# Low-rank attention and a feed-forward layer: attention of the next half batch between feed-forward matmuls, transposed, two heads per matmul, with loads that convert

## The chip, the cores and the metric

The kernel runs on one core of a Trainium2 chip. Time is device microseconds; the engines are PE (matmuls), ACT (activations), DVE (elementwise), POOL (here it issues the loads) and SP (it can issue transfers too). All inputs and the output are fp32; matmuls run in bf16 with fp32 sums.

## The reference

```python
batch, n_heads, seq, head_dim = (8, 8, 1024, 64);  k_proj = 64       # attention
n_tokens, d_model, d_ff = (8192, 512, 2048)                          # feed-forward

k_proj = np.einsum('ks,bhsd->bhkd', E, k)
v_proj = np.einsum('ks,bhsd->bhkd', F, v)
scores = scale * np.matmul(q, k_proj.transpose(0, 1, 3, 2))          # scale = 1/8
scores = scores - np.max(scores, axis=-1, keepdims=True)
attn = np.exp(scores)
attn = attn / (np.sum(attn, axis=-1, keepdims=True) + 1e-09)
attn_out = np.matmul(attn, v_proj)

x = attn_out.transpose(0, 2, 1, 3).reshape(B * S, H * D)
h = x @ w_in
g = h * (1.0 / (1.0 + np.exp(-1.702 * h)))
out = g @ w_out
```

## The kernel before, in words

It has two stages, one after the other. Stage one loops over the 8 batches. For each it loads Q, K and V in 8 chunks of 128 tokens (`kvf`, 256 KB each, all 8 heads side by side), converts each chunk to bf16 on DVE (`kvb`, L83, L103, L105), transposes Q per head on PE (L86, `qtb`), and sums K and V over the 1024 tokens against E and F (L106, L107, `kp_ps`, `vp_ps`). K's projection is transposed per head (`kpT`), V's gets a column of ones (`vp_ext`), which makes the softmax denominator come out of the same matmul. Then for each head and each half of the tokens (512): scores as 64 x 512 (L126), Exp on ACT (L129), the product with `vp_ext` (L131), a copy (L133), four transposes back to tokens on rows (L137), a reciprocal of the denominators (L140, 128 x 4), and a multiply into `x_all` (L143), which holds all 8192 tokens in SBUF.

Stage two loops over 16 blocks of 512 tokens: 16 transposes of `x_all` to `xT` (L160, L161); for each of 16 slices of the hidden layer four matmuls (L167) and one Gelu (L173) into `gT`; then 64 matmuls of the second layer (L176) into four PSUM banks, one copy of them on DVE (L183) and a 1 MB store (L184).

The weights are loaded in fp32 in stage one and converted on DVE (L60, L64). All transfers are issued by POOL, in one queue. The order on each engine is made by a scheduler from dependencies and buffer counts (most pools have two buffers, the PSUM pool of the second layer one).

Of the kernel before, what the change touches and what calls it, by code (L numbers as in the profile page):

```python
# [15 lines left out]

@with_exitstack
def kernel(ctx, tc, q, k, v, E, F,
                                                     moe_w_in, moe_w_out, out):
    nc = tc.nc  # L20
# [16 lines left out]
    ps_sm = ps_sm_ctx.__enter__()
# [3 lines left out]
    identf = consts.tile([P, P], F32)  # L41
    nc.vector.tensor_copy(identf, ident)

    ET = consts.tile([P, SC, KP], BF16)
    FT = consts.tile([P, SC, KP], BF16)
    w_in_sb = consts.tile([P, KC, DFF], BF16)
    w_out_sb = consts.tile([P, FC, DM], BF16)
    with tc.tile_pool(name="init", bufs=1) as init:
        for src, dst in [(E, ET), (F, FT)]:
            E_f = init.tile([KP, S], F32, name="ef_f32")  # L50
            nc.gpsimd.dma_start(out=E_f, in_=src)
            for sc in range(SC):
                ef_ps = ps_sm.tile([P, P], F32, name="sc_ps")
                nc.tensor.transpose(ef_ps[:, :KP], E_f[:, sc * P:(sc + 1) * P], identf[:KP, :KP])
                nc.vector.tensor_copy(dst[:, sc, :], ef_ps[:, :KP])
# [10 lines left out]
    x_all = consts.tile([P, NCHUNK, DM], BF16)

    GW = 4 * P

    ps_a_ctx = tc.tile_pool(name="ps_a", bufs=1, space=bass.MemoryType.PSUM)  # L70
    ps_a = ps_a_ctx.__enter__()
    for b in range(B):
        ci0 = b * SC
        qT = qpool.tile([D, H, S], BF16, name="qtb")
        qTv = qT.rearrange("d h (sc p) -> d h sc p", p=P)
        for sc in range(SC):
            qch_f = kvw.tile([P, H * D], F32, name="kvf")
            nc.gpsimd.dma_start(  # L78
                out=qch_f.rearrange("p (h d) -> p h d", h=H),
                in_=q[b, :, sc * P:(sc + 1) * P, :].transpose([1, 0, 2]),  # L80
            )
            qch = kvw.tile([P, H * D], BF16, name="kvb")
            nc.vector.tensor_copy(qch, qch_f)  # L83
            qt_ps = ps_sm.tile([D, H, P], BF16, name="qt_ps")
            for h in range(H):
                nc.tensor.transpose(qt_ps[:, h, :], qch[:, h * D:(h + 1) * D], ident)  # L86
            nc.vector.tensor_copy(qTv[:, :, sc, :], qt_ps)  # L87

        kp_ps = ps_a.tile([KP, H * D], F32, name="kp_ps")
        vp_ps = ps_a.tile([KP, H * D], F32, name="vp_ps")  # L90
        for sc in range(SC):
            kch_f = kvw.tile([P, H * D], F32, name="kvf")
            nc.gpsimd.dma_start(  # L93
                out=kch_f.rearrange("p (h d) -> p h d", h=H),
                in_=k[b, :, sc * P:(sc + 1) * P, :].transpose([1, 0, 2]),
            )
            vch_f = kvw.tile([P, H * D], F32, name="kvf2")
            nc.gpsimd.dma_start(  # L98
                out=vch_f.rearrange("p (h d) -> p h d", h=H),
                in_=v[b, :, sc * P:(sc + 1) * P, :].transpose([1, 0, 2]),  # L100
            )
            kch = kvw.tile([P, H * D], BF16, name="kvb")
            nc.vector.tensor_copy(kch, kch_f)  # L103
            vch = kvw.tile([P, H * D], BF16, name="kvb2")
            nc.vector.tensor_copy(vch, vch_f)  # L105
            nc.tensor.matmul(kp_ps, ET[:, sc, :], kch, start=(sc == 0), stop=(sc == SC - 1))  # L106
            nc.tensor.matmul(vp_ps, FT[:, sc, :], vch, start=(sc == 0), stop=(sc == SC - 1))  # L107

        vp_ext = work.tile([KP, H, D + 1], BF16, name="vp_ext")
        nc.vector.memset(vp_ext[:, :, D:D + 1], 1.0)  # L110
        kp_sb = work.tile([KP, H, D], F32, name="kp_sb")
        nc.vector.tensor_copy(kp_sb.rearrange("k h d -> k (h d)"), kp_ps)
        for h in range(H):
            nc.vector.tensor_copy(vp_ext[:, h, :D], vp_ps[:, h * D:(h + 1) * D])

        kpT_sb = work.tile([D, H, KP], BF16, name="kpT")
        for h in range(H):
            t_ps = ps_sm.tile([D, P], F32, name="qt_ps")
            nc.tensor.transpose(t_ps[:, :KP], kp_sb[:, h, :], identf[:KP, :KP])
            nc.vector.tensor_copy(kpT_sb[:, h, :], t_ps[:, :KP])  # L120

        for h in range(H):
            for sg in range(S // GW):
                col0 = sg * GW
                sc_ps = ps_sm.tile([KP, GW], F32, name="sc_ps")
                nc.tensor.matmul(sc_ps, kpT_sb[:, h, :], qT[:, h, col0:col0 + GW],  # L126
                                 start=True, stop=True)
                expT = small.tile([KP, GW], BF16, name="expT")
                nc.scalar.activation(expT, sc_ps, AF.Exp, scale=scale)  # L129
                out_ps = ps_sm.tile([D + 1, GW], F32, name="out_ps")  # L130
                nc.tensor.matmul(out_ps, vp_ext[:, h, :], expT, start=True, stop=True)  # L131
                out_sb = small.tile([D + 1, GW], F32, name="out_cp")
                nc.vector.tensor_copy(out_sb, out_ps)  # L133
                cg = GW // P
                ot_ps = ps_sm.tile([P, cg, D + 1], F32, name="qt_ps")
                for c in range(cg):
                    nc.tensor.transpose(ot_ps[:, c, :], out_sb[:, c * P:(c + 1) * P],  # L137
                                        identf[:D + 1, :D + 1])
                rden = small.tile([P, cg, 1], F32, name="rden")
                nc.vector.reciprocal(rden[:, :, 0], ot_ps[:, :, D])  # L140
                dst = x_all.rearrange("p n (h d) -> p h n d", h=H)[:, h, ci0 + sg * cg:ci0 + sg * cg + cg, :]
                a, bcast = bass.broadcast_tensor_aps(ot_ps[:, :, :D], rden)
                nc.vector.tensor_tensor(dst, a, bcast, op=ALU.mult)  # L143

    ps_a_ctx.__exit__(None, None, None)
    ps_sm_ctx.__exit__(None, None, None)
    ps_b_ctx = tc.tile_pool(name="ps_b", bufs=1, space=bass.MemoryType.PSUM)
    ps_b = ps_b_ctx.__enter__()
    ps_bt_ctx = tc.tile_pool(name="ps_bt", bufs=2, space=bass.MemoryType.PSUM)
    ps_bt = ps_bt_ctx.__enter__()  # L150
    ps_ht_ctx = tc.tile_pool(name="ps_ht", bufs=2, space=bass.MemoryType.PSUM)
    ps_ht = ps_ht_ctx.__enter__()
    gtpool = ctx.enter_context(tc.tile_pool(name="gtpool", bufs=1))
    NB = 4
    for cb in range(0, NCHUNK, NB):
        xT = work.tile([P, KC, NB, P], BF16, name="xT")
        for n in range(NB):
            for kc in range(KC):
                t_ps = ps_bt.tile([P, P], BF16, name="t_ps")
                nc.tensor.transpose(t_ps, x_all[:, cb + n, kc * P:(kc + 1) * P], ident)  # L160
                nc.vector.tensor_copy(xT[:, kc, n, :], t_ps)  # L161
        out_ps = ps_b.tile([P, NB, DM], F32, name="out_ps")
        gT = gtpool.tile([P, FC, NB, P], BF16, name="gT")
        for fc in range(FC):
            hT_ps = ps_ht.tile([P, NB, P], F32, name="hT_ps")
            for kc in range(KC):
                nc.tensor.matmul(  # L167
                    hT_ps,
                    w_in_sb[:, kc, fc * P:(fc + 1) * P],
                    xT[:, kc, :, :].rearrange("p n c -> p (n c)"),  # L170
                    start=(kc == 0), stop=(kc == KC - 1),
                )
# [48 lines left out]
```

## Time and profile before

| | us |
|---|---|
| median of 3 runs | 1149.72 (1147.58 to 1149.89) |
| span of the profiled execution | 1145.6 |
| runs' median less that span | 4.1 |
| PE busy | 886.1 (77%) |
| DVE busy | 387.3 (34%) |
| ACT busy | 230.9 (20%) |
| POOL busy | 200.7 (18%) |

No separate time of the profiled execution is given, so its span stands for it, and the 4.1 us for what lies around the span. A share of busy time is an average over two stages that are not alike: the view in 40 slices and the rows by stage tell them apart. A matmul's busy time overlaps that of its neighbours, so the rate of matmuls is read from their starts.

### The profile page before, as it was taken

What the parts mean: (1) busy time and instruction counts of PE and PEld (TensorE: products, weight loads), DVE (VectorE), ACT (ScalarE), POOL (GpSimd) and SP (SyncE); (2) the same over time, 40 slices, a digit from 0 to 9 for tenths busy, and PEclk for the clock granted to TensorE, in tenths of its full rate; (3) what the DMA queues carried; (4) which work ended last, traced back from release to release, by engine and by line L of the source; (5) the groups of instructions that cost most, each with busy time, mean ns of one, the idle gap of its engine ahead of it and who ended that gap; (6) DMA issues with size and microseconds to landing.
All of it is one profiled execution on the core that took longest, in us unless ns stands there. A gap on an engine that the chain in (4) does not pass through costs nothing.

```text
span 1145.6 us, 9870 instructions
## 1 busy us (share of the span) xinstructions
PE 886.1 (77%) x3746; PEld 405.3 (35%) x3792; DVE 387.3 (34%) x1093; ACT 230.9 (20%) x386; POOL 200.7 (18%) x236
## 2 busy tenths in 40 slices
PE   2377594867759486675898888998889988899886
PEld 1124141332414233241444333443334433344333
DVE  4456464564636456463601111011110111101110
ACT  0021020202102020111233311333113331133311
POOL 4532515143351514312000000000000000000000
PEclk9999995555555555555599899988899888998889
DMA  6752516244251524412000000000000010000000
GB/s 219 211 139 67 156 28 160 58 122 108 74 143 27 155 62 114 116 47 73 1 1 37 37 37 37 1 37 37 37 37 1 37 37 37 37 1 37 37 37 37
DMA packets 21775, 76.67 MB, mean 67 GB/s; under 512 B 3680, under 2 KB 3680, under 8 KB 21216
## 3 DMA queue, kind: packets, MB, share of 16 engines
q0 software_dynamic: 21728, 76.04, 22.8%
q8 instruction: 30, 0.49, 0.2%
q14 instruction: 17, 0.14, 0.0%
HBM read 59.24 MB, written 16.78 MB: 66 GB/s over the span
## 4 chain that ended last, share of the span: by engine, by line
issue 37%; PE 36%; DMA 15%; DVE 7%; ACT 3%; POOL 1%; POOLq 0%; ACTq 0%; DVEq 0%
DMA kvf<-in_k_dram 10%; PE hT_ps L167 8%; PE out_ps L176 7%; PE sc_ps L126 6%; PE out_ps L131 5%; PE qt_ps L86 3%; PE qt_ps L137 3%; ACT expT L129 3%; DMA kvf<-in_q_dram 2%; DMA wtmp<-in_moe_w_in_dram 1%; DVE qtb L87 1%; DVE kvb L103 1%; DMA wtmp<-in_moe_w_out_dram 1%; PE vp_ps L107 1%; PE t_ps L160 1%
## 5 line engine op out<-in xcount | busy, mean ns | idle before, releaser
L167 PE MATMUL hT_ps<-xT,w_in_sb 128*128 128x512 bf16 x999 | 252.5, 414 | 2.0 <-issue 0.9
L173 ACT ACTIVATE gT<-hT_ps 128x512 bf16<-128x512 f32 x256 | 152.8, 597 | 407.4 <-PE hT_ps L167 404.2
L176 PE MATMUL out_ps<-w_out_sb,gT 128*128 128x512 bf16 x1003 | 222.5, 379 | 1.1
L183 DVE COPY out_sb<-out_ps 128x2048 f32<-128x2048 f32 x16 | 36.7, 2291 | 458.8 <-PE out_ps L176 458.8
L129 ACT ACTIVATE expT<-sc_ps 64x512 bf16<-64x512 f32 x128 | 75.5, 590 | 484.5 <-PE sc_ps L126 373.1
L167 PEld LDWEIGHTS <-w_in_sb 128*128 128x128 bf16 x1024 | 107.3, 105 | 145.0 <-issue 45.3
L176 PEld LDWEIGHTS <-gT 128*128 128x128 bf16 x1024 | 100.2, 98 | 120.8
L184 POOL DMA_DIRECT2D out_dram<-out_sb x16 | 12.1, 753 | 597.5 <-DVE xT L161 562.9
L78 POOL DMA_DIRECT2D kvf<-in_q_dram x64 | 58.5, 914 | 240.0 <-DVE kvb L83 193.4
L86 PE MATMUL qt_ps<-ident,kvb 128*64 128x128 bf16 x512 | 65.6, 307 | 42.1 <-DVE kvb L83 40.0
L137 PE MATMUL qt_ps<-identf,out_cp 65*128 65x65 f32 x512 | 88.5, 328 | 5.7 <-DVE rden L140 4.1
L160 PE MATMUL t_ps<-ident,x_all 128*128 128x128 bf16 x256 | 50.0, 248 | 55.1 <-DVE xT L161 53.7
L106 PE MATMUL kp_ps<-kvb,ET 128*64 128x512 bf16 x64 | 37.7, 589 | 67.1 <-DVE kvb L103 67.1
L133 DVE COPY out_cp<-out_ps 65x512 f32<-65x512 f32 x128 | 84.7, 663 | 8.2 <-PE out_ps L131 8.1
L137 PEld LDWEIGHTS qt_ps<-identf,out_cp 65*128 65x128 f32 x512 | 64.7, 215 | 60.8 <-PE sc_ps L126 29.6
L131 PE MATMUL out_ps<-expT,vp_ext 64*65 64x512 bf16 x128 | 81.0, 632 | 0.0
L86 PEld LDWEIGHTS <-kvb 128*64 128x64 bf16 x512 | 52.2, 164 | 78.4 <-DVE kvb L83 68.8
L126 PE MATMUL sc_ps<-qtb,kpT 64*64 64x512 bf16 x128 | 75.0, 610 | 6.2 <-ACT expT L129 0.3
L107 PE MATMUL vp_ps<-kvb,FT 128*64 128x512 bf16 x64 | 37.5, 586 | 53.8 <-DVE kvb L105 53.4
L93 POOL DMA_DIRECT2D kvf<-in_k_dram x64 | 58.0, 906 | 64.8 <-DVE kvb L103 46.6
L87 DVE COPY qtb<-qt_ps 64x1024 bf16<-64x1024 bf16 x64 | 43.6, 681 | 48.9 <-PE qt_ps L86 48.5
L98 POOL DMA_DIRECT2D kvf<-in_v_dram x64 | 58.9, 920 | 1.7 <-issue 1.0
(36 smaller groups left out, 373.9 us busy)
## 6 DMA issues: line engine op xcount, KB each, us to landing
kvf<-in_q_dram POOLq DMA_DIRECT2D x64, 256.0 KB, 3.8
kvf<-in_v_dram POOLq DMA_DIRECT2D x64, 256.0 KB, 4.1
kvf<-in_k_dram POOLq DMA_DIRECT2D x64, 256.0 KB, 3.8
out_dram<-out_sb POOLq DMA_DIRECT2D x16, 1024.0 KB, 4.7
wtmp<-in_moe_w_in_dram POOLq DMA_DIRECT2D x4, 1024.0 KB, 5.5
wtmp<-in_moe_w_out_dram POOLq DMA_DIRECT2D x16, 256.0 KB, 3.0
ef_f<-in_E_dram POOLq DMA_DIRECT2D x1, 256.0 KB, 3.7
ef_f<-in_F_dram POOLq DMA_DIRECT2D x1, 256.0 KB, 4.3
```

The costliest lines, as they stand in the source:

```text
L78: nc.gpsimd.dma_start(out=qch_f.rearrange("p (h d) -> p h d", h=H), in_=q[b, :, sc * P:(sc + 1) * P, :].transpose([1, 0, 2]),)
L86: nc.tensor.transpose(qt_ps[:, h, :], qch[:, h * D:(h + 1) * D], ident)
L98: nc.gpsimd.dma_start(out=vch_f.rearrange("p (h d) -> p h d", h=H), in_=v[b, :, sc * P:(sc + 1) * P, :].transpose([1, 0, 2]),)
L126: nc.tensor.matmul(sc_ps, kpT_sb[:, h, :], qT[:, h, col0:col0 + GW], start=True, stop=True)
L129: nc.scalar.activation(expT, sc_ps, AF.Exp, scale=scale)
L131: nc.tensor.matmul(out_ps, vp_ext[:, h, :], expT, start=True, stop=True)
L133: nc.vector.tensor_copy(out_sb, out_ps)
L137: nc.tensor.transpose(ot_ps[:, c, :], out_sb[:, c * P:(c + 1) * P], identf[:D + 1, :D + 1])
L160: nc.tensor.transpose(t_ps, x_all[:, cb + n, kc * P:(kc + 1) * P], ident)
L167: nc.tensor.matmul(hT_ps, w_in_sb[:, kc, fc * P:(fc + 1) * P], xT[:, kc, :, :].rearrange("p n c -> p (n c)"), start=(kc == 0), stop=(kc == ...
L173: nc.scalar.activation(gT[:, fc, :, :].rearrange("p n c -> p (n c)"), hT_ps, AF.Gelu_apprx_sigmoid)
L176: nc.tensor.matmul(out_ps[:, n, :], gT[:, fc, n, :], w_out_sb[:, fc, :], start=(fc == 0), stop=(fc == FC - 1),)
```

## The change

The two stages become one loop. The parts:

- The loads convert: `k_sb`, `v_sb`, `q_sb`, `ef_sb` and both weights are bf16 tiles that POOL's transfers fill from fp32. A partition now holds 8 consecutive tokens (`(p j)`), so K and V arrive in rows of 2 KB and Q, split by `j`, in rows of 256 bytes. K and V of a batch are one transfer each, 2 MB; Q is 8 transfers.
- K's projection goes to PSUM partitions 0 to 63 and V's to 64 to 127 of one tile. They are written in blocks on the diagonal of `kbd` and `vbd`, two heads each, the rest being zeros. One matmul with 128 rows then serves two heads.
- Attention stays transposed (channels on rows): scores, Exp, then two matmuls on the same Exp tile, one with `ones2` (blocks of ones) which puts the denominator on all 64 rows of its head (`d_ps`), and one with `vbd` (`n_ps`). A reciprocal of 128 x 512 and a multiply give `xT` directly; `x_all` and its transposes are gone.
- The order is written by hand (`manual_schedule`). A block's 24 slots are its 16 first-layer groups and 8 halves of second-layer outputs; `fill` names what of the next half batch's attention follows each slot. An even block does `proj` after slots 1 to 4, `proj_out` after 5, `q_tr` after 8, 10, 12, 14; all blocks but the last ones do `scores` after 16, 18, 20, 22 and `outp` after 0, 6, 12, 17. Batch 0's attention, and the first half of its `outp`, run ahead of the loop.
- The second layer has one PSUM bank per 128 tokens, copied by ACT; the stores go out on SP's queue, by block.

```diff
+    ps_h = ctx.enter_context(tc.tile_pool(name="ps_h", bufs=2, space=PSUM))
+    ps_o = ctx.enter_context(tc.tile_pool(name="ps_o", bufs=2, space=PSUM))
+    ps_s = ctx.enter_context(tc.tile_pool(name="ps_s", bufs=2, space=PSUM))
+    ps_n = ctx.enter_context(tc.tile_pool(name="ps_n", bufs=1, space=PSUM))
+    ctx.enter_context(tc.manual_schedule())
...
+    def load_kv(b, parts=1):
+        kt[b] = ldpool.tile([P, H, J, D], BF16, name="k_sb")
+        vt[b] = ldpool.tile([P, H, J, D], BF16, name="v_sb")
+        hs = H // parts
+        for i in range(parts):
+            for src, dst in ((k, kt[b]), (v, vt[b])):
+                nc.gpsimd.dma_start(
+                    out=dst[:, i * hs:(i + 1) * hs],
+                    in_=src[b, i * hs:(i + 1) * hs].rearrange("h (p j) d -> p h j d", p=P))
+    def load_q(b):
+        qt[b] = ldpool.tile([P, J, H, D], BF16, name="q_sb")
+        qv = q[b].rearrange("h (p j) d -> p j h d", p=P)
+        for j in range(J):
+            nc.gpsimd.dma_start(out=qt[b][:, j], in_=qv[:, j])
...
+    load_kv(0, parts=2)
+    load_q(0)
...
+    def proj(b, j):
+            for e, src in ((0, kt[b]), (1, vt[b])):
+                nc.tensor.matmul(kvps[b][e * KP:(e + 1) * KP], eft[:, e, j, :], src[:, :, j, :],
+                                 start=(j == 0), stop=(j == J - 1))
+    def proj_out(b):
+            nc.vector.tensor_copy(k_b, ps[:KP])
+            vv = ps[KP:].rearrange("k (p t) d -> k p t d", t=2)
+            nc.vector.tensor_copy(vbd[:KP, :, :D], vv[:, :, 0, :])
+            nc.vector.tensor_copy(vbd[KP:, :, D:], vv[:, :, 1, :])
+            for p in range(HP):
+                nc.tensor.transpose(t_ps[:, p, :], k_b[:, 2 * p:2 * p + 2, :].rearrange("k t d -> k (t d)"),
+                                    ident[:KP, :KP])
+            nc.vector.tensor_copy(kbd[:D, :, :KP], t_ps[:D])
+            nc.vector.tensor_copy(kbd[D:, :, KP:], t_ps[D:])
+    def q_tr(b, g):
+            t_ps = ps_s.tile([P, 2, HP, P], BF16, name="s_ps")
+            for jj in range(2):
+                for p in range(HP):
+                    nc.tensor.transpose(
+                        t_ps[:, jj, p, :],
+                        qt[b][:, 2 * g + jj, 2 * p:2 * p + 2, :].rearrange("s t d -> s (t d)"), ident)
+            nc.vector.tensor_copy(qT[b][:, :, 2 * g:2 * g + 2, :],
+                                  t_ps.rearrange("r j p s -> r p j s"))
+    def scores(h, p):
+            s_ps = ps_s.tile([P, TB], F32, name="s_ps")
+            nc.tensor.matmul(s_ps, kbds[b % 2][:, p, :],
+                             qT[b][:, p, c * JB:(c + 1) * JB, :].rearrange("r j s -> r (j s)"),
+                             start=True, stop=True)
+            nc.scalar.activation(expT[h][:, p, :], s_ps, AF.Exp, scale=scale)
+    def outp(h, p):
+            d_ps = ps_n.tile([P, TB], F32, name="d_ps")
+            nc.tensor.matmul(d_ps, ones2, expT[h][:, p, :], start=True, stop=True)
+            n_ps = ps_n.tile([P, TB], F32, name="n_ps")
+            nc.tensor.matmul(n_ps, vbds[b % 2][:, p, :], expT[h][:, p, :], start=True, stop=True)
+            rden = att.tile([P, TB], F32, name="rden")
+            nc.vector.reciprocal(rden, d_ps)
+            nc.vector.tensor_tensor(xT[h][:, p, :], n_ps, rden, op=ALU.mult)
...
+    def ffn1(j, fc):
+        h_ps = ps_h.tile([P, TB], F32, name="h_ps")
+        for kc in range(KC):
+            nc.tensor.matmul(h_ps, w_in_sb[:, kc, fc * P:(fc + 1) * P], xT[j][:, kc, :],
+                             start=(kc == 0), stop=(kc == KC - 1))
+        nc.scalar.activation(gts[j][:, fc, :], h_ps, AF.Gelu_apprx_sigmoid)
+    def ffn2(j, n, half):
+        for fc in range(half * FC // 2, (half + 1) * FC // 2):
+            nc.tensor.matmul(o_ps[0], gts[j][:, fc, n * P:(n + 1) * P], w_out_sb[:, fc, :],
+                             start=(fc == 0), stop=(fc == FC - 1))
+        if half == 1:
+            nc.scalar.copy(osb[j][:, n, :], o_ps[0])
...
+    for b in range(1, B):
+        j0 = NB2 * b
+        for j in range(J):
+            at(j0 - 2, 1 + j // 2, proj(b, j))
+        at(j0 - 2, 5, proj_out(b))
+        for g in range(J // 2):
+            at(j0 - 2, 8 + 2 * g, q_tr(b, g))
+        for c in range(NB2):
+            for p in range(HP):
+                at(j0 + c - 2, 16 + 2 * p, scores(j0 + c, p))
+    for h in range(1, NBLK):
+        for p, slot in enumerate((0, 6, 12, 17)):
+            at(h - 1, slot, outp(h, p))
...
+    load_kv(1)
+    load_q(1)
+    for j in range(NBLK):
+        if j % NB2 == 0 and j // NB2 + 2 < B:
+            load_kv(j // NB2 + 2)
+            load_q(j // NB2 + 2)
+        for fc in range(FC):
+            ffn1(j, fc)
+            for f in fill.pop((j, fc), []):
+                f()
+        for s in range(2 * JB):
+            ffn2(j, s // 2, s % 2)
+            for f in fill.pop((j, FC + s), []):
+                f()
```

How the order moves, first on PE. Before, at the end of stage one: the last product with `vp_ext`, the transposes back, and then the transposes of `x_all` that open stage two:

```order
L131 MATMUL out_ps<-expT,vp_ext 65x512 [waits Activation_49]
L137 MATMUL qt_ps<-identf,out_cp 128x65 [waits DVE_49,PE_49]
L137 MATMUL qt_ps<-identf,out_cp 128x65 x3
...
L160 LDWEIGHTS x_all [waits DVE_49]
L160 MATMUL t_ps<-ident,x_all 128x128 [waits PE_49]
...
L167 LDWEIGHTS w_in_sb
L167 MATMUL hT_ps<-xT,w_in_sb 128x512
```

Now, at the start of block 0 (L184 is the first layer, L168 and L170 `outp`, L112 `proj`, of batch 1):

```order
L184 LDWEIGHTS w_in_sb
L184 MATMUL h_ps<-xT,w_in_sb 128x512 [waits DVE_49]
L168 LDWEIGHTS ones_86
L168 MATMUL d_ps<-expT,ones_86 128x512
L170 LDWEIGHTS vbd_91
L170 MATMUL n_ps<-expT,vbd_91 128x512
...
L112 LDWEIGHTS eft [waits DMASW6_49]
L112 MATMUL s_ps<-k_sb,eft 64x512 [waits Activation_49]
L112 LDWEIGHTS eft
L112 MATMUL s_ps<-v_sb,eft 64x512 [waits DMASW7_49]
```

Attention's matmuls moved from ahead of all feed-forward to between its groups, and `proj` of batch 1 waits there, in PE's queue, for batch 1's K and V.

On ACT, before: all 128 Exp, one table load, all Gelu:

```order
L129 ACT_TABLE_LOAD
L129 ACTIVATE expT<-sc_ps 64x512 [waits PE_49] x2
L129 ACTIVATE expT<-sc_ps 64x512 [waits PE_49,Activation_49] x126
L173 ACT_TABLE_LOAD [waits DMASW4_49,DMASW3_49,DMASW5_49,DMASW2_49,DMASW6_49,DMASW1_49,DMASW7_49,DMASW0_49]
L173 ACTIVATE gT<-hT_ps 128x512 [waits PE_49] x16
```

Now, from the second half of block 1 into block 2 (L158 is Exp, L200 the copy of the second layer's output, L186 Gelu):

```order
L158 ACT_TABLE_LOAD [waits PE_49]
L158 ACTIVATE expT<-s_ps 128x512 [waits Activation_49]
L200 COPY o_sb<-o_ps 128x512 [waits PE_49]
...
L158 ACTIVATE expT<-s_ps 128x512 [waits PE_49]
L200 COPY o_sb<-o_ps 128x512 [waits PE_49]
L186 ACT_TABLE_LOAD [waits PE_49]
L186 ACTIVATE gT<-h_ps 128x512 [waits Activation_49]
L186 ACTIVATE gT<-h_ps 128x512 [waits PE_49] x15
L158 ACT_TABLE_LOAD
```

Exp moved in between the Gelus of two blocks, with a table load on either side; the one ahead of Gelu carries the wait for PE.

On POOL's queue, before: weights, Q, V and K in turn, in pieces of 256 KB to 1 MB:

```order
L59 DMA wtmp<-in_moe_w_in_dram 128x2048
L63 DMA wtmp_157<-in_moe_w_out_dram 128x512
L78 DMA kvf<-in_q_dram 128x8x64 x2
L59 DMA wtmp<-in_moe_w_in_dram 128x2048
L63 DMA wtmp_160<-in_moe_w_out_dram 128x512
```

Now, from the program's start (L73 is K and V, L81 Q, L91 and L94 the weights; the last three rows are batch 1's):

```order
L83 DMA ef_sb<-in_E_dram 64x1024
L84 DMA ef_sb<-in_F_dram 64x1024
L73 DMA k_sb<-in_k_dram 128x4x512
L73 DMA v_sb<-in_v_dram 128x4x512
L73 DMA k_sb<-in_k_dram 128x4x512
L73 DMA v_sb<-in_v_dram 128x4x512
L81 DMA q_sb<-in_q_dram 128x8x64 x8
L91 DMA w_in_sb<-in_moe_w_in_dram 128x4x512 x4
L94 DMA w_out_sb<-in_moe_w_out_dram 128x4x512 x4
L73 DMA k_sb<-in_k_dram 128x8x512
L73 DMA v_sb<-in_v_dram 128x8x512
L81 DMA q_sb<-in_q_dram 128x8x64 x8
```

Both weights moved ahead of batch 1's K and V, in whole, where before they came in pieces between the batches' chunks.

More of the change, by code (lines that the diff above doesn't have):

```diff
@@ L66 @@
[L66 to L143, printed above, removed]
```

167 lines of the change are left out of this document (95 added, 72 removed).

## The prediction

> **What bounds the kernel now.** I read the page's 40 slices first, then busy time in the two stages, then the waits, then one block of the second stage in order of time.
>
> ```profile
> span 1145.6 us, 9870 instructions
> PE   2377594867759486675898888998889988899886
> PEclk9999995555555555555599899988899888998889
> DMA  6752516244251524412000000000000010000000
> ```
>
> The slices show two halves that never overlap: loads only in the left one, a full TensorE clock from slice 20 on. The split is the end of attention, at 567 us. In the next rows, the columns are PE, weight loads, DVE, ACT and POOL busy, clock, DMA share, GB/s:
>
> ```profile
> 0.00:567.00 567.00, 373.78 (x1488) 172.77 (x1488) 304.95 (x821) 78.09 (x130) 188.67 (x220) 0.66 0.39 105
> 567.00:1145.60 578.60, 512.31 (x2258) 232.49 (x2304) 82.34 (x273) 152.83 (x256) 12.05 (x16) 0.91 0.08 30
> ```
>
> In the first 567 us no engine is full (DVE 305, PE 374 at a low clock). The waits say why:
>
> ```profile
> ACT expT L129 <- PE out_ps L131: 111.4, 95, 2.9
> DVE kvb L103 <- DMA kvf<-in_k_dram: 67.2, 52, 2.6
> PE kp_ps L106 <- DVE kvb L103: 67.1, 59, 2.5
> ```
>
> It is a chain of short hand-overs between PE, ACT, DVE and the loads, each waiting for the other. In the second half PE is the bound. One block of 512 tokens:
>
> ```profile
> 645.53 12.16 PE L167 MATMUL hT_ps<-xT,w_in_sb 128*128 128x512 bf16 x52
> 657.53 13.98 PE L176 MATMUL out_ps<-w_out_sb,gT 128*128 128x512 bf16 x63
> 671.34 0.28 PE L160 MATMUL t_ps<-ident,x_all 128*128 128x128 bf16 x2
> 671.54 2.29 DVE L183 COPY out_sb<-out_ps 128x2048 f32<-128x2048 f32 x1 [29.38 <-PE out_ps L176]
> ...
> 676.67 0.35 PE L160 MATMUL t_ps<-ident,x_all 128*128 128x128 bf16 x2 [0.18 <-DVE xT L161]
> 677.79 6.39 PE L167 MATMUL hT_ps<-xT,w_in_sb 128*128 128x512 bf16 x22
> ```
>
> The 64 second-layer matmuls start at 657.53 and the next work at 671.34: 13.8/64 = 0.216 us each, with no gap at the change from the first layer. Then PE waits for DVE's big copy and for 16 small transposes, and the next block starts cold: 22 matmuls in 6.39 us where 22 x 0.216 = 4.75.
>
> **The change, part by part.** Removed: the separate attention stage (567 us), the transposes and cold starts between blocks, the 2.29 us copies from PE's path (ACT now copies, 512 columns at a time). The new kernel is a loading and attention prologue for batch 0, then 16 blocks in which PE runs 128 feed-forward matmuls with the next half batch's attention between them. I price the blocks, then the prologue. Rows of the groups; behind the first bar stand busy us and the mean ns of one:
>
> ```profile
> L173 ACT ACTIVATE gT<-hT_ps 128x512 bf16<-128x512 f32 x256 | 152.8, 597 | 407.4 <-PE hT_ps L167 404.2 <-remote 3.2
> L133 DVE COPY out_cp<-out_ps 65x512 f32<-65x512 f32 x128 | 84.7, 663 | 8.2 <-PE out_ps L131 8.1
> L131 PE MATMUL out_ps<-expT,vp_ext 64*65 64x512 bf16 x128 | 81.0, 632 | 0.0
> L143 DVE TENSOR_TENSOR x_all<-qt_ps,rden 128x256 bf16<-128x256 f32 x128 | 52.5, 411 | 0.1
> L87 DVE COPY qtb<-qt_ps 64x1024 bf16<-64x1024 bf16 x64 | 43.6, 681 | 48.9 <-PE qt_ps L86 48.5
> L140 DVE RECIPROCAL rden<-qt_ps 128x4 f32<-128x4 f32 x128 | 23.2, 181 | 71.2 <-PE qt_ps L137 68.0
> L129 ACT ACT_TABLE_LOAD x1 | 1.3, 1283 | 0.7 <-PEq L205 0.7
> L55 DVE CAST ET<-sc_ps 128x64 bf16<-128x64 f32 x8 | 1.4, 220 | 3.9 <-PE sc_ps L54 3.9
> ```
>
> Eight transposes, cold, run in 1.06 us, 0.13 each:
>
> ```profile
> 15.57 1.06 PE L86 MATMUL qt_ps<-ident,kvb 128*64 128x128 bf16 x8 [0.65 <-DVE kvb L83]
> ```
>
> *PE per block.* Feed-forward: 128 x 0.216 = 27.6 us. Fill of an even block (0 to 12, seven of them): 8 matmuls of `outp`, 4 of `scores`, 16 of `proj` at 0.216 (6.0), 32 transposes of `q_tr` at 0.1 (3.2; between half the cold 0.13 and all of it, 2.1 to 4.2), four in `proj_out` (0.3): 37.2 us. An odd block (1 to 13) has only `outp` and `scores`: 27.6 + 12 x 0.216 = 30.2. Block 14 has `outp` alone, 29.3; block 15 nothing, 27.6. For the fill I take the cadence of the feed-forward, since operands are ready ahead; the bound above is a lone matmul's 0.632 (L131), the bound below zero for half of `proj`, whose K and V results go to different PSUM partitions and might run together (-1.7 us per even block).
>
> *DVE.* The reciprocal grows from 128x4 to 128x512, a size that no row shows. 220 ns for 64 columns and 411 for 256 give 1.0 ns per column and 156 fixed; the reciprocal's 181 leaves 25 for 4 columns, 6.3 each, so 3.4 us for 512. Bounds: 0.67 (one pass) and, the whole 181 taken as per-column cost, 23. I take 3.4, since fixed cost is common to these rows. With the multiply (0.67) and hand-overs one `outp` holds DVE 4.3 us. The closest two are six first-layer groups apart, 6 x 0.86 + 0.43 = 5.6 us, so `d_ps` and `n_ps`, single buffers, are free in time. In even blocks `q_tr`'s copies (0.68 each, L87) queue behind a reciprocal, but the same of the two PSUM buffers is asked for again only four groups later. I cost DVE at nothing; its cover is those 5.6 us.
>
> *ACT.* Exp and Gelu now alternate in each block: a table load (1.28 us) ahead of the first Exp and one ahead of the first Gelu, which waits for that block's first group of matmuls. The first Gelu then ends at 0.9 + 1.3 + 0.6 + 0.1 = 2.9 us, and PE needs its PSUM buffer for group 2. In an even block PE gets there at 3.0 (two groups, `outp`, one slot of `proj`): hidden. In odd ones at 2.16: 0.85 us lost, in blocks 3, 5, ..., 13 and 14, seven times. The Exp load hides behind second-layer matmuls.
>
> *Blocks:* 7 x 37.2 + 7 x 30.2 + 29.3 + 27.6 + 7 x 0.85 = 260.4 + 211.4 + 56.9 + 6.0 = 534.7, say 535 us.
>
> *Prologue and loads.* All loads stay on POOL's queue, in fp32, converted on the way. Sizes and rates:
>
> ```profile
> kvf<-in_q_dram POOLq DMA_DIRECT2D x64, 256.0 KB, 3.8
> out_dram<-out_sb POOLq DMA_DIRECT2D x16, 1024.0 KB, 4.7
> wtmp<-in_moe_w_in_dram POOLq DMA_DIRECT2D x4, 1024.0 KB, 5.5
> wtmp<-in_moe_w_out_dram POOLq DMA_DIRECT2D x16, 256.0 KB, 3.0
> ef_f<-in_E_dram POOLq DMA_DIRECT2D x1, 256.0 KB, 3.7
> ```
>
> ```profile
> 20.00:60.00 40.00, 13.26 (x64) 6.66 (x62) 18.39 (x35) 0.00 (x0) 21.32 (x28) 1.00 0.77 224
> 200.00:400.00 200.00, 139.63 (x555) 64.24 (x554) 110.53 (x297) 28.32 (x48) 68.00 (x75) 0.51 0.37 98
> 646.00:682.00 36.00, 32.27 (x146) 14.76 (x148) 5.14 (x17) 9.92 (x17) 0.75 (x1) 0.95 0.08 30
> ```
>
> Block 0 needs batch 1's K and V after its second group, and they stand behind everything else: E and F 512 KB, batch 0's K, V, Q 3 x 2048, weights 2 x 4096, then 2 x 2048: 18,944 KB, 19.4 MB. Rate over share gives what full engines would move: 224/0.77 = 291 GB/s, 98/0.37 = 265, 30/0.08 = 375. No row shows a converting transfer, so I take the lowest, 265, and keep half of it (132) and 375 as ends. Then K and V of batch 1 land at 1.3 (first issue) + 73 + 2.5 = 77 us. The compute of the prologue ends earlier: batch 0's K and V at 21, `proj` 16 x 0.43 cold (28), `proj_out` (31), `q_tr` and its last copy (36), eight Exp at 0.65 (41), four `outp` at 4.3 (59). PE does 2.2 us of block 0 and waits until 77. Later batches, 6.3 MB in 24 us, have 67 us each: hidden.
>
> *End:* a copy of 0.6 us and a 256 KB store; the old one took 6.2 us from issue to the span's end for 1 MB, so 5.4.
>
> ```profile
> 1136.82 2.29 DVE L183 COPY out_sb<-out_ps 128x2048 f32<-128x2048 f32 x1 [28.34 <-PE out_ps L176]
> 1139.41 0.75 POOL L184 DMA_DIRECT2D out_dram<-out_sb  x1 [34.59 <-DVE out_sb L183]
> ```
>
> **Sum.** 77 + (535 - 2.2) + 2 (cold restart after the wait, from the 1.6 above) + 6 = 618 us of span. The median of the runs, 1149.7, lies 4.1 above the profiled span of 1145.6; with the same 4.1: 622 us, 0.54 of before.
>
> **Rivals.**
>
> *A table switch costs more than its load's row* (0.13). The two loads in this trace stand at idle times, so what follows one is not seen. If ACT were held another 1.4 us, about a second load, the first Gelu would end at 4.2: even blocks 2 to 12 lose 1.2, the seven odd ones 1.4 more: +17 us, 639. Against it: ACT has only some 17 us of work in a block of 33 (24 instructions of 0.6 and the two loads). The Trainium skill, ScalarE: Activation LUTs, What ACT_TABLE_LOAD costs, gives a 1283 ns load, with which the row agrees exactly, and a drain of about 1380 ns behind it, and says to batch functions by set; by that page the time would be this rival's. No run here shows the drain.
>
> *Fill matmuls don't run at the cadence* (0.08). If each of some 22 fill places in a pair of blocks exposes half of 0.632 - 0.216, that is 4.6 us per pair, +32: 654. For it: every place adds a wait in PE's in-order queue. Against: no gap at 657.53.
>
> *Converting transfers run at plain speed or better* (0.17). Above 19.4 MB / (59 - 4) = 353 GB/s compute sets the start: block 0 begins at 59 and has no wait: 59 + 535 + 6 + 4 = 604. A faster reciprocal on top (0.67) takes 11 more: 593. On the reciprocal, the Trainium skill, VectorE: DVE Perf Modes, Walkthrough: the 8-slice pipeline in each mode, has it iterate with a repeat count of 8; at that page's 0.96 GHz an estimate is 4.4 us, the trace's 6.3 ns per column being a little less; by it this rival's 604 would be 608.
>
> *They run at half speed* (0.13): 132 GB/s, batch 1 at 151 us, 622 + 74 = 696; a later batch takes 48 us and still hides.
>
> *Slower than before* (0.02): converting packets so slow that loads bound the whole run.
>
> ```profile
> HBM read 59.24 MB, written 16.78 MB: 66 GB/s over the span
> ```
>
> After the last batch lands, four blocks and the end remain, 135 us; so it decides below 59.24 MB / (1150 - 135) = 58 GB/s; at 50 the time is 1320. For it: no row rules it out. Against: 256-byte rows, the worst here, moved 98 GB/s at a third of the engines.
>
> **How the numbers follow.** My forecast, the start set by loads at about 265 GB/s and PE-bound blocks, has 0.47 and by its own terms reaches from 605 to 640 (the transposes +-7, `proj` -12, rate 300 to 230). With the plain-speed rival, the table rival and the fill rival, 0.85 lie in 593 to 685; half speed and slower stay out. Faster by over 0.2%, which is about what a measurement of this kernel can tell from no change: 0.975; within it 0.005; slower 0.02.
>
> **What the new profile would show.** PE busy with no gap above a microsecond from about 80 us on, clock near 1; block pairs some 68 us apart. `s_ps` matmuls of batch 1 waiting for `in_k_dram` or `in_v_dram` until about 77 us. RECIPROCAL near 3.4 us. PE waiting under 1 us for ACT at group 2 of odd blocks, and for DVE nowhere in the blocks. DMA share high up to 85 us, then about a third. Wrong it would be if the share stays high with GB/s low (conversion), or if PE idles at each fill place.

## The result, and the profile after

The changed kernel takes 582.01 us (median of 4 runs, 581.44 to 582.58), against 1149.81 for the kernel before: a ratio of 0.5066, 95% interval 0.5056 to 0.5075. The direction was right; the time lies 40 us under the forecast of 622, and 11 under the range's lower end of 593. One of the six runs of the single-table kernel further down took 960 us at a granted clock of 0.56 and is not in its ratio.

The page of the changed kernel, span, slices and queues:

```profile
span 580.8 us, 6222 instructions
PE   0635999999999999999999999999999999999997
PEclk9966999999999999999999999999999999999999
DMA  9999999029900691019910493010010101010001
GB/s 141 181 206 190 191 191 149 2 73 165 111 14 1 142 148 73 0 74 149 72 69 1 111 171 82 1 73 1 0 73 1 73 0 73 0 73 1 37 36 73
q0 software_dynamic: 87616, 29.63, 45.7%
HBM read 59.24 MB, written 16.78 MB: 131 GB/s over the span
```

A slice is 14.5 us. From slice 4 on (58 us) PE is full at full clock, where before the left half had one such slice (slice 5). Two rows want care. POOL's queue (`q0`) counts 29.63 MB, while HBM was read for 59.24: the counter and the GB/s row tell what was *written*, in bf16, and twice as much was read, in fp32. So "206" in slice 2 is 412 GB/s of source bytes.

The steady part in one row (PE, weight loads, DVE, ACT, POOL busy, clock, DMA share, GB/s):

```profile
200.00:580.00 380.00, 369.85 (x1819) 168.57 (x1853) 191.85 (x126) 185.78 (x291) 24.51 (x28) 1.00 0.31 58
```

PE is busy for 97% of it, DVE for 50%, ACT for 49%. The groups and waits that the prediction spoke of (mean ns of one before the second bar, idle time behind it; in the waits: us in total, times, longest):

```profile
L172 DVE RECIPROCAL rden<-d_ps 128x512 f32<-128x512 f32 x64 | 214.8, 3356 | 184.3 <-PE d_ps L168 179.7
L184 PE MATMUL h_ps<-xT,w_in_sb 128*128 128x512 bf16 x1000 | 243.9, 383 | 10.0 <-ACT gT L186 6.6
L186 ACT ACT_TABLE_LOAD x15 | 19.2, 1283 | 4.2 <-PE h_ps L184 4.2
```

```profile
PE s_ps L112 <- DMA k_sb<-in_k_dram: 9.0, 1, 9.0
PE d_ps L168 <- DVE rden L172: 8.6, 3, 3.2
PE h_ps L184 <- ACT gT L186: 6.6, 14, 0.7
PE s_ps L112 <- DMA v_sb<-in_v_dram: 5.7, 2, 3.8
```

Every wait of PE for DVE lies in the prologue: three between its four `outp` (8.6 us), some short ones, and the last, 2.19 us, in the first group of block 0, for the fourth `outp`. Behind that group there is none. PE's order of time at the places on which the sum rested:

```profile
47.43 0.58 PE L184 MATMUL h_ps<-xT,w_in_sb 128*128 128x512 bf16 x1 [2.19 <-DVE xT L173]
50.50 0.40 PE L112 MATMUL s_ps<-k_sb,eft 128*64 128x512 bf16 x1
54.67 0.59 PE L112 MATMUL s_ps<-v_sb,eft 128*64 128x512 bf16 x1 [3.76 <-DMA v_sb<-in_v_dram]
...
57.43 0.64 PE L112 MATMUL s_ps<-k_sb,eft 128*64 128x512 bf16 x1
57.43 0.63 PE L112 MATMUL s_ps<-v_sb,eft 128*64 128x512 bf16 x1
57.86 0.63 PE L112 MATMUL s_ps<-k_sb,eft 128*64 128x512 bf16 x1
...
90.15 1.03 PE L184 MATMUL h_ps<-xT,w_in_sb 128*128 128x512 bf16 x4
...
120.95 1.03 PE L184 MATMUL h_ps<-xT,w_in_sb 128*128 128x512 bf16 x4
...
126.47 0.40 PE L112 MATMUL s_ps<-k_sb,eft 128*64 128x512 bf16 x1
126.47 0.40 PE L112 MATMUL s_ps<-v_sb,eft 128*64 128x512 bf16 x1
126.71 0.38 PE L112 MATMUL s_ps<-k_sb,eft 128*64 128x512 bf16 x1
...
127.03 1.04 PE L184 MATMUL h_ps<-xT,w_in_sb 128*128 128x512 bf16 x4
...
132.77 0.61 PE L141 MATMUL s_ps<-ident,q_sb 128*128 128x128 bf16 x8
133.22 1.89 PE L184 MATMUL h_ps<-xT,w_in_sb 128*128 128x512 bf16 x7
...
156.14 1.03 PE L184 MATMUL h_ps<-xT,w_in_sb 128*128 128x512 bf16 x4
...
157.44 1.03 PE L184 MATMUL h_ps<-xT,w_in_sb 128*128 128x512 bf16 x4
159.19 4.48 PE L184 MATMUL h_ps<-xT,w_in_sb 128*128 128x512 bf16 x20 [0.73 <-ACT gT L186]
...
187.25 1.03 PE L184 MATMUL h_ps<-xT,w_in_sb 128*128 128x512 bf16 x4
```

Read from top to bottom: the first layer of block 0 starts in full at 47.43 (three of its matmuls ran ahead, at 43.75, and the fourth waited for the prologue's last `outp`); PE stands from 50.90 to 54.67 for batch 1's V; block 0 ends at 90.15, block 1 at 120.95, block 2 (even) at 156.14, block 3 (odd) at 187.25. So an even block takes 35.19 us and an odd one 31.11. After the stall, the pairs of `proj` (57.43, 57.86) step at 0.43 us where later ones step at 0.24 (126.47, 126.71): a cold PE, with a granted clock of 0.50 from 54 to 60 us.

### The profile page after: what moved, and what is told of

Same layout as the page of the kernel before. It is cut to its first block, busy times and chain, and to the rows that moved or that the text cites. A ratio compares the mean times of both kernels' runs of the same rounds, so it can differ in the third digit from the quotient of the medians.

```text
span 580.8 us, 6222 instructions
## 1 busy us (share of the span) xinstructions
PE 534.1 (92%) x2621; PEld 241.4 (42%) x2672; DVE 297.5 (51%) x209; ACT 264.9 (46%) x414; POOL 79.1 (14%) x98
## 3 DMA queue, kind: packets, MB, share of 16 engines
q0 software_dynamic: 87616, 29.63, 45.7%
HBM read 59.24 MB, written 16.78 MB: 131 GB/s over the span
## 4 chain that ended last, share of the span: by engine, by line
PE 85%; DMA 8%; ACT 5%; POOL 1%; issue 1%; ACTq 0%; POOLq 0%
PE o_ps L197 38%; PE h_ps L184 37%; DMA v_sb<-in_v_dram 6%; ACT L186 3%; PE s_ps L112 2%; PE s_ps L141 2%; PE s_ps L155 2%; PE n_ps L170 2%; DMA w_in_sb<-in_moe_w_in_dram 2%; PE d_ps L168 2%; ACT gT L186 1%; PE s_ps L127 0%; POOL k_sb L73 0%; ACT o_sb L200 0%; POOL q_sb L81 0%
## 5 line engine op out<-in xcount | busy, mean ns | idle before, releaser
L172 DVE RECIPROCAL rden<-d_ps 128x512 f32<-128x512 f32 x64 | 214.8, 3356 | 184.3 <-PE d_ps L168 179.7
L184 PE MATMUL h_ps<-xT,w_in_sb 128*128 128x512 bf16 x1000 | 243.9, 383 | 10.0 <-ACT gT L186 6.6
L197 PE MATMUL o_ps<-w_out_sb,gT 128*128 128x512 bf16 x1002 | 233.4, 379 | 1.2
L186 ACT ACTIVATE gT<-h_ps 128x512 bf16<-128x512 f32 x256 | 151.3, 597 | 131.8 <-PE h_ps L184 131.7
L184 PEld LDWEIGHTS <-w_in_sb 128*128 128x128 bf16 x1024 | 97.4, 98 | 130.7 <-issue 25.1
L158 ACT ACTIVATE expT<-s_ps 128x512 bf16<-128x512 f32 x64 | 37.8, 597 | 88.1 <-PE s_ps L155 87.3
L200 ACT COPY o_sb<-o_ps 128x512 f32<-128x512 f32 x64 | 37.4, 585 | 86.0 <-PE o_ps L197 83.1
L81 POOL DMA_DIRECT2D q_sb<-in_q_dram x64 | 56.1, 902 | 79.9 <-PE s_ps L141 39.9
L173 DVE TENSOR_TENSOR xT<-n_ps,rden 128x512 bf16<-128x512 f32 x64 | 44.3, 692 | 6.7
L73 POOL DMA_DIRECT2D k_sb<-in_k_dram x9 | 7.7, 860 | 183.9 <-PE s_ps L112 181.3
L168 PE MATMUL d_ps<-expT,ones 128*128 128x512 bf16 x59 | 23.2, 394 | 8.6 <-DVE rden L172 8.6
L112 PE MATMUL s_ps<-k_sb,eft 128*64 128x512 bf16 x64 | 22.2, 437 | 9.0 <-DMA k_sb<-in_k_dram 9.0
L112 PE MATMUL s_ps<-v_sb,eft 128*64 128x512 bf16 x64 | 22.0, 440 | 5.7 <-DMA v_sb<-in_v_dram 5.7
L170 PE MATMUL n_ps<-expT,vbd 128*128 128x512 bf16 x64 | 25.1, 393 | 0.9 <-DVE xT L173 0.6
L155 PE MATMUL s_ps<-qT,kbd 128*128 128x512 bf16 x64 | 24.3, 380 | 1.4 <-ACT expT L158 0.8
```

The lines of the kernel that those rows point to most:

```text
L81: nc.gpsimd.dma_start(out=qt[b][:, j], in_=qv[:, j])
L112: nc.tensor.matmul(kvps[b][e * KP:(e + 1) * KP], eft[:, e, j, :], src[:, :, j, :], start=(j == 0), stop=(j == J - 1))
L155: nc.tensor.matmul(s_ps, kbds[b % 2][:, p, :], qT[b][:, p, c * JB:(c + 1) * JB, :].rearrange("r j s -> r (j s)"), start=True, stop=True)
L158: nc.scalar.activation(expT[h][:, p, :], s_ps, AF.Exp, scale=scale)
L170: nc.tensor.matmul(n_ps, vbds[b % 2][:, p, :], expT[h][:, p, :], start=True, stop=True)
L172: nc.vector.reciprocal(rden, d_ps)
```

## The experiments

The kernels ran in three groups, each with the kernel before beside it, so ratios to before, with their 95% intervals, are what I compare across groups. 0.001 of the ratio is 1.15 us. First the changed kernel again, as the base of the first group:

> The changed kernel again, beside its variants on one chip. Every theory: 582 us, K and V of batch 1 landing at 50 to 55 us, even blocks 35.2 us apart, odd ones 31.1.

It took 582.24 us, 0.507 (0.5055 to 0.5084). In its profiled execution (584.07 us) V of batch 1 landed at 56.59, later than the 50 to 55 expected, where the first had 54.67, with the same order of loads: 1.9 us between two executions of one kernel.

**When batch 1's loads are issued.** Batch 1's K, V and Q go ahead of `w_out` in POOL's queue:

```diff
         nc.gpsimd.dma_start(out=w_in_sb[:, :, sl], in_=w_in_v[:, :, sl])
+    load_kv(1)
+    load_q(1)
     for i in range(4):
         sl = slice(i * FC // 4, (i + 1) * FC // 4)
         nc.gpsimd.dma_start(out=w_out_sb[:, sl, :], in_=w_out_v[:, sl, :])
...
     for p in range(HP):
         outp(0, p)()
-    load_kv(1)
-    load_q(1)
```

> K, V and Q of batch 1 are issued ahead of the second layer's weights. If loads set the start (K and V of batch 1 at 50.5 and 54.7 us, at about 410 GB/s of fp32), they land 10 us earlier, PE passes slot 1 of block 0 without the 4 us wait and is warm sooner: 576 to 578 us, and compute (the fourth outp, first layer at 47.4) sets the start. Rival, compute already sets it: 582. Rival, the weights of the second layer now come too late for slot 16: over 582.

576.52 us, 0.5017 (0.5004 to 0.5031). PE of this kernel no longer waits at the first `proj`:

```profile
47.65 0.59 PE L186 MATMUL h_ps<-xT,w_in_sb 128*128 128x512 bf16 x1 [2.19 <-DVE xT L175]
50.73 0.64 PE L114 MATMUL s_ps<-k_sb,eft 128*64 128x512 bf16 x1
```

So the loads set the pace of block 0, as the prediction said, but by only some 4 us of waiting and a colder PE behind it: block 1 of this kernel starts at 84.09, against 90.15, and the two profiled executions differ by the same 6.06 (576.52 and 582.58). No wait for `w_out` appears, though it now lands later.

**The prologue's compute.** A copy stands in for the reciprocal, so the softmax is not normalised in this kernel:

```diff
-            nc.vector.reciprocal(rden, d_ps)
+            nc.vector.tensor_copy(rden, d_ps)
```

> A copy takes the reciprocal's place (0.7 us for 3.36; the softmax is left unnormalised). If DVE is hidden in the blocks and loads set the start, the prologue's outp chain ends 10 us earlier and PE waits for K and V of batch 1 all the same: 581 to 582. Rival, DVE costs PE something in every block: 0.5 us each or more, 574 or less.

582.66 us, 0.5073 (0.5062 to 0.5084): nothing. The first layer was ready ten microseconds earlier (37.21, against 47.43), and PE only waited longer:

```profile
37.21 0.38 PE L184 MATMUL h_ps<-xT,w_in_sb 128*128 128x512 bf16 x1 [0.37 <-DVE xT L173]
...
50.10 0.64 PE L112 MATMUL s_ps<-k_sb,eft 128*64 128x512 bf16 x1 [11.22 <-DMA k_sb<-in_k_dram]
...
55.16 0.58 PE L112 MATMUL s_ps<-v_sb,eft 128*64 128x512 bf16 x1 [4.42 <-DMA v_sb<-in_v_dram]
```

This does two things. Inside the blocks DVE's 60 reciprocals are hidden (a price of nothing was right), and the four of the prologue are hidden by the loads alone. Both edits together, the earlier load and the copy (softmax not normalised), should then give what neither gives:

> Batch 1's loads ahead of the second layer's weights, and a copy in place of the reciprocal (softmax unnormalised). If loads set the start once compute is shortened, K and V of batch 1 land at about 45 us and nothing else holds block 0: some 8 to 10 us below the changed kernel, 572 to 574, where each of the two edits alone gives 577 and 582. Rival, the gain of the two is only that of the first: 577.

571.94 us, 0.4982 (0.4973 to 0.4991), 10 us below the changed kernel; the loads are the later ones again, 10 us earlier:

```profile
44.54 0.59 PE L114 MATMUL s_ps<-v_sb,eft 128*64 128x512 bf16 x1 [5.38 <-DMA v_sb<-in_v_dram]
```

V's landing moved from 54.67 to 44.54, 10.1 us, by taking the 4.19 MB of `w_out` out of its way: 414 GB/s of source bytes. POOL's issuing is not what sets this pace: in the changed kernel it issued batch 1's V at 30.00 us, 24.7 us ahead of the landing, and between the issues that follow it waited 1.2 to 4.2 us for transfers under way.

**What a converting transfer costs.** `w_in` is loaded as fp32, unconverted, into the buffers of `gT`, and ACT casts it before the first block:

```diff
-        nc.gpsimd.dma_start(out=w_in_sb[:, :, sl], in_=w_in_v[:, :, sl])
+        if i % 2 == 0:
+            stage = work.tile([P, 2, KC, DFF // 4], F32, name="gT")
+        nc.gpsimd.dma_start(out=stage[:, i % 2], in_=w_in_v[:, :, sl])
+        casts.append((w_in_sb[:, :, sl], stage[:, i % 2]))
...
+    for dst, w_f in casts:
+        nc.scalar.copy(dst, w_f)
     for p in range(HP):
         outp(0, p)()
```

> The first layer's weights are loaded in fp32, unconverted, and converted by ACT. If a converting transfer goes at the pace of the fp32 bytes it reads, as a plain one does, K and V of batch 1 land where they did (54.7) and the time is 582 within 1.5. If conversion is what makes it fast, since half the bytes are written, 4.2 MB at 265 GB/s take 16 us for 10 and the time is 587 to 589. If conversion slows it, V lands earlier and the time is 578 to 580.

582.54 us, 0.5074 (0.5065 to 0.5082), and V's wait ends at 55.31, between the 54.67 and 56.59 of the unchanged order: no difference. The rows in 40 slices of 0.4 us, for 20 to 36 us, first of the changed kernel, then of this one:

```profile
GB/s 154 155 154 155 154 155 173 188 204 203 212 207 202 207 205 210 205 207 210 207 200 205 207 207 205 205 205 205 205 205 215 197 205 207 212 207 205 212 202 200
```

```profile
GB/s 156 155 154 155 155 162 317 414 399 471 379 440 369 420 369 369 420 358 399 410 348 399 410 358 420 369 369 420 358 389 420 348 341 261 205 210 207 207 210 205
```

On the left of both is Q, in rows of 256 bytes: 155 written, 310 read. Then `w_in`: converting 205 written, 410 read; plain about 390, written and read. On the right of the second row `w_out`, converting, returns to 205. A converting transfer of these sizes thus runs at the pace of the fp32 bytes it reads; the cast costs nothing, and saves nothing but SBUF and an engine's copy.

**K and V side by side.** All eight K products first, then all eight V products, two tokens' positions at a time, so that a slot's four matmuls write the same half of the PSUM partitions:

```diff
-    def proj(b, j):
+    def proj(b, i):
...
-            for e, src in ((0, kt[b]), (1, vt[b])):
+            e, src = ((0, kt[b]), (1, vt[b]))[i // (J // 2)]
+            for j in (2 * i % J, 2 * i % J + 1):
```

> Batch b's K products now all come before its V products (slots 1 and 2 K, slots 3 and 4 V), so that a K and a V product no longer stand next to each other. If neighbours that write PSUM partitions 0-63 and 64-127 run side by side, as their equal start times say, each proj slot grows from 0.64 us to 4 x 0.216 + 0.16 = 1.02, an even block from 35.2 to 36.7, seven of them +10.7 us; V of batch 1 is asked for two slots later, so block 0 loses its wait for V of some 4 us: 589 us. Rival, the equal starts are an artefact of the records and each product costs 0.216 either way: even blocks stay at 35.2 and the time falls by the 4 us of block 0, 578.

587.54 us, 0.5115 (0.5103 to 0.5128); the changed kernel in the same group 582.24. PE of this kernel, V's wait, the start of block 1, and block 2:

```profile
55.32 1.02 PE L113 MATMUL s_ps<-v_sb,eft 128*64 128x512 bf16 x4 [1.14 <-DMA v_sb<-in_v_dram]
...
85.82 1.03 PE L185 MATMUL h_ps<-xT,w_in_sb 128*128 128x512 bf16 x4
...
116.62 1.03 PE L185 MATMUL h_ps<-xT,w_in_sb 128*128 128x512 bf16 x4
...
120.83 1.05 PE L113 MATMUL s_ps<-k_sb,eft 128*64 128x512 bf16 x4
121.81 1.04 PE L185 MATMUL h_ps<-xT,w_in_sb 128*128 128x512 bf16 x4
...
153.30 1.03 PE L185 MATMUL h_ps<-xT,w_in_sb 128*128 128x512 bf16 x4
```

Block 2 takes 36.68 us (116.62 to 153.30), 1.49 more than side by side. A slot of four is 0.98 here (120.83 to 121.81), and 0.56 in the changed kernel (126.47 to 127.03), where K's and V's products start in the same hundredth of a microsecond. The six even blocks from 2 to 12 lose 6 x 1.49 = 8.9, but block 0 gains: V is now asked for two slots later, PE waits for it 1.1 us and not 3.8, and block 1 starts 4.3 us earlier (85.82 against 90.15). 8.9 - 4.3 = 4.6 is what separates the two profiled executions, 587.15 and 582.58.

**The table switches.** Gelu's function stands in for Exp, so only the first table load is left, and the attention weights are other numbers than Exp's:

```diff
-            nc.scalar.activation(expT[h][:, p, :], s_ps, AF.Exp, scale=scale)
+            nc.scalar.activation(expT[h][:, p, :], s_ps, AF.Gelu_apprx_sigmoid, scale=scale)
```

> Gelu's function stands in for Exp in attention (its values are wrong for it), so that ACT never switches tables. If the switches cost only what the trace shows, 14 waits of PE for ACT with 6.6 us in all: 575. Rival, a switch also holds ACT some 1.4 us after its load: 23 us less, 559.

574.53 us, 0.5002 (0.4995 to 0.501): 7.8 us by the ratios. The waits come to the same: in the changed kernel the third first-layer group starts late by 0.6 us in block 1, by 0.9 in blocks 3, 5, ..., 13 and 14, and by 0.2 in blocks 2, 4, ..., 12, about 8 in all. If the thirty loads of 1.28 us (15 for Gelu, 15 for Exp) had lain on the path, it would have been 38. The same without a change of the result: a Gelu of one column directly behind the block's last Exp, so that Gelu's table is loaded during the second layer:

```diff
+    def early_table():
+        nc.scalar.activation(warm_o, warm, AF.Gelu_apprx_sigmoid)
...
             for p in range(HP):
                 at(j0 + c - 2, 16 + 2 * p, scores(j0 + c, p))
+            at(j0 + c - 2, 22, early_table)
```

> A Gelu of one column per row directly after a block's last Exp brings Gelu's table in while PE is in the second layer; the result is unchanged. If PE's waits for ACT at the third group are the table load alone, they all go: 575. Rival, they come from ACT being late for another reason: 582.

573.98 us, 0.4999 (0.4991 to 0.5008). It gives all that a single table gives. ACT of this kernel at the end of block 2, and its first-layer group, whose idle time was 10.0 us:

```profile
154.89 1.28 ACT L212 ACT_TABLE_LOAD   x1
156.19 0.20 ACT L212 ACTIVATE warm_o<-warm 128x1 f32<-128x1 f32 x1
...
156.87 0.60 ACT L186 ACTIVATE gT<-h_ps 128x512 bf16<-128x512 f32 x1
```

```profile
L184 PE MATMUL h_ps<-xT,w_in_sb 128*128 128x512 bf16 x1024 | 244.0, 383 | 2.2 <-DVE xT L173 2.2
```

**Both useful edits.** The earlier load of batch 1 and the early table, nothing else:

> Batch 1's loads ahead of the second layer's weights, and the Gelu of one column after a block's last Exp. The gains of the two alone, 5.7 and 8.3 us, are in different places, so they should add: 568. Rival, the wait for ACT was what the earlier start ran into: 572 or more.

569.58 us, 0.4957 (0.4946 to 0.4968): 0.0113 below the first group's base, the sum of the two parts (0.0053 and 0.0071) within the intervals.

**The cold start.** On top of that, 48 matmuls whose results nothing reads, between the prologue's `outp`:

```diff
+    def keep_warm(n):
+        w_ps = ps_h.tile([P, TB], F32, name="h_ps")
+        for i in range(n):
+            nc.tensor.matmul(w_ps, kbds[0][:, 0, :], qT[0][:, 0, :JB, :].rearrange("r j s -> r (j s)"),
+                             start=True, stop=True)
     for p in range(HP):
         outp(0, p)()
+        keep_warm((8, 12, 14, 14)[p])
```

> As the one before, with 48 more matmuls of 512 columns, whose results nobody reads, between and after batch 0's outp. Block 0 then starts at full clock where before its first 10 us or so ran at 0.43 us a matmul: 3 to 5 us less, 563 to 565. Rival, the idle time in the prologue is too short for them and they delay outp or the first layer: 568 or more.

567.41 us, 0.4937 (0.4929 to 0.4946), 2.2 us less than 569.58 in the same group, and the best of all. Stretches of the two kernels, first without, then with those matmuls:

```profile
31.00:47.00 16.00, 4.86 (x11) 1.06 (x9) 15.48 (x8) 1.76 (x2) 4.24 (x5) 0.63 1.51 195
47.00:62.00 15.00, 14.52 (x70) 5.26 (x70) 9.75 (x9) 5.37 (x9) 8.35 (x10) 0.83 1.50 196
```

```profile
31.00:47.00 16.00, 12.93 (x58) 5.46 (x57) 15.22 (x7) 2.07 (x3) 4.25 (x6) 1.00 1.52 194
47.00:62.00 15.00, 14.98 (x88) 6.16 (x87) 11.75 (x12) 6.57 (x11) 8.34 (x10) 1.00 1.48 196
```

The granted clock went from 0.63 and 0.83 to 1.00 in both, as expected, but the gain was half of what I had put down. DVE is busy 15.2 to 15.5 of the 16 us ahead of the first block in both kernels (four reciprocals and multiplies of 4.06 each), so block 0 cannot begin much sooner; a warm PE only shortens its first microseconds. Without the extra matmuls the clock was back at 1.00 at 52.1 us, some 5 us into block 0, and not after the 10 that I had assumed. In the 15 us from 47 on, 70 matmul records became 88.

## Why the prediction was wrong

The direction was right, and so were the two bounds, loads for the start of block 0 and PE for the blocks; the sizes were not. Put against the profiled execution (582.58 us, a span of 580.8), the terms of the sum are:

| term | predicted | measured | difference |
|---|---|---|---|
| K and V of batch 1 landed | 77 | 54.67 | -22.3 |
| block 0 behind that wait | 37.2 - 2.2 + 2 | 35.48 | -1.5 |
| block 1 | 30.2 | 30.80 | +0.6 |
| blocks 2 to 15 | 467.3 | 455.8 | -11.5 |
| last copy and store | 6 | 4.1 | -1.9 |
| outside the span | 4.1 | 1.8 | -2.3 |

They add up to 38.9 of the 39.4 us; the rest is rounding in the sum. The last term was no property of the kernel: every run, of the kernel before too, lies 1.8 us above its own span (1147.77 and 1146.0, for one), and 4.1 came of a median set against the span of another run.

**The step that failed** is the rate: "No row shows a converting transfer, so I take the lowest, 265". 19.4 MB landed in 54.67 - 1.3 us, 363 GB/s on average. Three rows had given 265, 291 and 375, and the choice of the lowest had only caution behind it; 375, kept as an upper end, would have put K and V at 55.5, within a microsecond. The row of 265 came from a stage of mixed small transfers, mostly rows of 256 bytes, at a third of the engines. What held the batch up in the new kernel is 2 KB rows, at 410 GB/s read, and Q's 256-byte rows, at 310, and the experiment with a plain `w_in` shows that conversion takes nothing from this. The rate alone would not have been enough: with 375 the sum comes to some 600, still above the range's lower end, and the 18 us left are for the most part the blocks (11.5) and the two terms at the end (4.2).

**The prologue's compute** was a second error, which the forecast hid since it took the loads as the later ones, but which made the plain-speed rival's 604 too high. The chain was put at 59 and ended at 47.43: its terms were K and V at 21 (17.42), `proj` at 6.9 (about 3.4, K and V side by side), `q_tr` at 5 (3.7 on PE) and each `outp` at 4.3 (4.06). With 47.4 that rival would have been decided by the loads, near 54.67, as it was. The range's lower end of 593 had a start of 48, near the measured 47.43, but by luck: it came from a reciprocal of 0.67 us, where it took 3.36. What kept the measured time outside is that from there to the end of block 15 the kernel takes 529.3 us, the wait for V included, where the rival had 535, and that the two terms at the end are 5.9 and not 10.

**The blocks.** An odd block was 30.2 + 0.85 = 31.05 by the sum and 31.11 by the trace; PE comes to group 2 at 157.44 + 0.86 = 158.30 and starts at 159.19, 0.89 later. The even block was 37.2 and is 35.19. Two sizes were off, and a stall was missing. I took 0.1 us for a transpose, between half the cold 0.13 and all of it: eight take 0.45 (132.77 to 133.22), 0.056 each, so 1.8 us in a block and not 3.2. And I saw that K and V "might run together (-1.7 us per even block)" and left it out of the sum. Set apart, a slot and the group behind it take 0.98 + 0.97, more than the 8 x 0.216 = 1.73 of the sum, so that the change from full to half outputs costs about 0.2 by itself; side by side they take 0.56 + 0.96. Against the sum that is 0.2 a slot, 0.8 in a block. With a stall of 0.2 us for ACT at group 2 (PE gets there 2.8 us into the block, and the first Gelu ends at 3.0), -1.4 - 0.8 + 0.2 = -2.0.

Block 1 was put at 30.2 and took 30.80. The sum counted a table load before Gelu in blocks 3, 5, ..., 13 and 14, but block 0 has Exp in its last slots too, so block 1 pays one as well: PE comes to its group 2 at 91.44 + 0.86 = 92.30 and starts at 92.89, 0.59 later. It is less than in block 3 since the load here starts at 90.95, 0.80 us into the block and not 1.11.

**What held.** The cadence of 0.216 for the fill (no gap at any fill place but the waits for ACT, so that rival fell); DVE costed at nothing, shown by the copy in place of the reciprocal; the reciprocal itself, 3.356 against 3.4, closer than a step from 4 columns to 512 could promise. For this the Trainium skill, VectorE: DVE Perf Modes, Walkthrough: the 8-slice pipeline in each mode, led to an estimate of 4.4; the measurement decides for the lower one, which was scaled from the trace.

**The table rival fell.** Gelu starts as soon as its table is loaded; ACT of the changed kernel, at the start of block 1 and of block 3:

```profile
90.35 0.58 ACT L200 COPY o_sb<-o_ps 128x512 f32<-128x512 f32 x1 [1.13 <-PE o_ps L197]
90.95 1.28 ACT L186 ACT_TABLE_LOAD   x1
...
156.34 0.58 ACT L200 COPY o_sb<-o_ps 128x512 f32<-128x512 f32 x1 [1.13 <-PE o_ps L197]
157.25 1.28 ACT L186 ACT_TABLE_LOAD   x1 [0.32 <-PE h_ps L184]
158.54 1.09 ACT L186 ACTIVATE gT<-h_ps 128x512 bf16<-128x512 f32 x2
```

157.25 + 1.28 = 158.53, and the Gelu starts at 158.54. The drain of about 1380 ns that the Trainium skill (ScalarE: Activation LUTs, What ACT_TABLE_LOAD costs) puts with each switch does not stand behind the load here, nor ahead of it: in block 1 the load starts 0.02 us after the copy's end at 90.93 (in block 3, where it waits for PE, 0.33 after). The advice of the same page of the Trainium skill (section Table sets: the hidden batching unit), to batch activation calls by set, still was worth 8 us here, of which the prediction's sum had 6.0 as a cost.

**The cold stretch, and what is left open.** In slices of 0.2 us the granted clock of the changed kernel rises to 1.00 at 50.5 us, falls to 0.50 at 53.9, near the end of the stall, and rises at 60.8. With the plain `w_in` it rises at 52.0, falls at 55.5 and rises at 58.9. After nearly the same stall (3.76 and 3.71 us) PE is thus cold for 6.8 us in one and 3.4 in the other, and all these steps lie about 3.4 us apart or twice that. So the same stall can cost one such step at half clock or two; what sets the steps is open.

## What to carry to other kernels

Price a transfer that converts by the bytes it reads, and take the rate from a row of like row size (2 KB rows with 2 KB rows), not from the busy share of a mixed stage. When two chains run up to the same start, here loads and prologue compute, cost both with equal care and try both at once: one alone showed nothing or 6 us, and the pair 10. Where PE is full, put half-width matmuls next to each other so that neighbours write different halves of a PSUM tile, and put a table load where the engine that waits for it is still busy with something else.

## What the runs showed of the hardware

- POOL's converting transfers moved 205 GB/s as written, 410 as read, with rows of 2 KB, and 155 and 310 with rows of 256 bytes; a plain one in the same place moved about 390. While they run, the profile's DMA share stands above 1 (1.5 in the stretches above; 1.27 for `w_in` converting, 1.03 for `w_in` plain), so share is no measure of how full the engines are there.
- Two matmuls with 64 output rows each, to the lower and the upper half of one PSUM tile, started together: four in 0.56 us side by side, 0.98 on the same half. The Trainium skill, TensorEngine Tiling (Array Packing), Overview, states up to 2x for such a pair; the slots here give 1.75.
- A transpose of 128 x 128 in bf16, at full clock and in a row of eight, took 0.056 us.
- After a stall of 3.8 us matmuls stepped at 0.43 us, and at 0.216 again 6 us later; after one of 3.7 us in another kernel the clock was back within 3.4 us of its fall.
- A table load followed the copy ahead of it by 0.02 us, and the Gelu behind it started 0.01 us after its end.
